# Dealing the first 713 steps of a fused attention and expert kernel anew to five queues

## The chip, the cores and the metric

The kernel runs on one core of one Trainium2 chip. A core has five engines, each with an instruction queue of its own that it works through in order: TensorE (PE, matrix products), VectorE (DVE), ScalarE (ACT), GpSimd (POOL) and SyncE (SP, which issues transfers here). ACT and POOL issue transfers too. All transfers run on the core's 16 DMA engines. Matrix products are written to PSUM banks, and DVE or ACT must read a bank before another product may overwrite it. The metric is the device time of one execution in microseconds.

## The reference

There are two stages. First a linear attention over q, k and v of shape 8 x 8 x 576 x 64 (batch, heads, sequence, width), then a mixture of 4 experts that every one of the 4608 tokens passes through.

```python
phi = lambda x: np.where(x > 0, x, np.exp(x) - 1.0) + 1.0
kv = np.einsum('bhsd,bhse->bhde', phi(k), v)
z = np.sum(phi(k), axis=2)
num = np.einsum('bhsd,bhde->bhse', phi(q), kv)
den = np.einsum('bhsd,bhd->bhs', phi(q), z)[..., None] + 1e-06
x = (num / den).transpose(0, 2, 1, 3).reshape(4608, 512)
p = domain_probs / (domain_probs.sum(-1, keepdims=True) + 1e-09)
for e in range(4):                      # w1: 4 x 512 x 1024, w2: 4 x 1024 x 512
    out += p[:, e:e + 1] * (np.maximum(x @ w1[e], 0.0) @ w2[e])
```

## The kernel before

The tokens are worked on in 9 tiles of 512. Tile j below 8 is the first 512 positions of batch j; the last 64 positions of all eight batches ("left-overs") make tile 8. Batch j+1's attention is computed beside tile j's experts. Only for batch 0 is there nothing to run beside it, so its attention, at the very start, is cut into many small pieces.

The work is a set of named steps. Each is a function or a generator; a generator yields between its parts, and each part belongs to one engine. The names that matter here, a digit i being the pair of heads or the quarter:

- batch 0's attention: `lq`, `lk`, `lv` load (line 548 and line 540; `CFG["LQ"]` and its like say which engine issues; lq3 and lk0 are ACT's, the others SP's). `ke`, `qe` are the exponentials on ACT (lines 563 and 581), `kl`, `ql` the linear part (566, 584) and `km`, `qm` the minimum of both (570, 587) on DVE, ql2 on POOL. `vc` casts v (573: vc0 and vc3 on POOL, vc1 on DVE, vc2 on ACT). `kv` is the 64 x 65 product (606) and two copies out of PSUM (617). `qT` turns phi(q) by PE and copies it on ACT (597). `nd` is numerator and denominator (628) and their quotient on DVE (631, 632). `xT` turns the result (642) and copies it (644).
- `L` with a group of hidden columns and a token half: expert 0's first layer of tile 0, two products of four matmuls (655), then a relu on ACT (664).
- `warm0` to `warm4`: 14, 3, 2, 1 and 5 matmuls on zeros (997), which keep PE busy while it would wait. They are the fillers.
- `w` with layer, expert and part: a weight's load with a cast, issued by POOL (lines 224 to 230). `k`, `v`, `q` with a digit: raw loads of batch 1 by POOL (319). `rk`, `rv`: its left-overs, in two halves (297).
- `p1` to `p7` and `c22`, with tile, expert and half: a block of a first layer, done with seven products instead of eight. p1 writes bank b, ACT copies it to a bank e; p2 adds to e, and ACT takes the relu of it (901); p5 overwrites the same bank e; p6 and p7 add to b, with copies to `u2` and `u3` on ACT (879); c22 adds u3 to e on DVE (852); p3 adds to e, p4 to b. `s` and `t` are the sums of weights that they need (DVE), `ts` the sums of tokens (DVE for tile 0, POOL for later ones).
- `y` with expert, token quarter and part: the second layer of tile 0 (715); `m` with tile and expert: that of later tiles, also by seven products (810), for which `hs` on POOL makes hidden sums (777 to 783).
- `b1.` and `b2.`: the attention of batches 1 and 2, with `b1.k0` and its like the two parts of phi on ACT (344, 347), `km`, `qm` the minimum on DVE (352), `v0` a cast of v on ACT (357), `lk`, `lv`, `lq` the left-overs (375 to 381), `kv`, `qT`, `nd`, `xT` as above. `load` and `next` are loads that SP issues.

Each of four tags has two PSUM banks, and u3 has a single buffer.

What sets the order: `CFG["EARLY"]` is a text of names. `advance` (line 1107) takes each name in turn and runs the step's next part, whose instructions go to the end of their engine's queue. So the text is dealt to five queues, and only the order within one queue has an effect, with the buffers' turns. After the text, at the start of expert 0 of tile 2, all that is left follows by due positions that the change leaves alone. A name that stands two or three times is one step's successive parts; below a prime marks the second part (qT0' is the copy of qT0) and two the third.

Of the kernel before, what the change touches and what calls it, by code (L numbers as in the profile page):

```python
# [84 lines left out]
    "WARM": (14, 3, 2, 1, 5),  # L85
    "BANK": {'qT0': 'py', 'qT1': 'b', 'nd00': 'py', 'nd00+': 'b', 'kv2': 'py', 'xT00': 'b', 'kv3': 'b', 'nd10+': 'b', 'L00': 'b', 'L10': 'py', 'nd01': 'b', 'xT01': 'py', 'nd11+': 'b', 'L20': 'e', 'L30': 'e', 'L01': 'e', 'L11': 'py', 'L21': 'py', 'L31': 'b', 'b1.qT3': 'py', 'b1.nd30': 'py', 'b1.nd21': 'b', 'b1.q1': 'b', 'b1.qT1': 'py', 'b1.nd01': 'py', 'b1.xT2': 'b', 'b1.nd11': 'py', 'b1.xT0': 'b'},
    "EARLY": (
# [31 lines left out]
    ),  # L119
}  # L120

# [1029 lines left out]
```

## Time and profile before

| | us |
|---|---|
| median of 3 runs | 485.68 (485.55 to 485.99) |
| the profiled execution | 485.38 |
| its span, first to last instruction | 483.6 |
| PE busy in the span | 474.8 |
| end of the part that the text orders, on PE | 117.8 |
| mean granted TensorE clock | 0.997 |

Engine rows give busy time, its share and the number of instructions. Timeline rows give start and length in microseconds, engine, line, operation, output and inputs with their shapes, and in brackets how long the engine had been idle and what ended that. A DMA row's length is its issue alone; when the data land is recorded apart. PE's rows overlap: the next matmul starts before the last has left the array.

### The profile page before, as it was taken

The page shows a single profiled execution, that of the slowest core. Times are in us where ns is not written, and L with a number is a line of the kernel's source. Part 1 is how long each engine was busy: PE and PEld are TensorE (multiplying, and loading weights), DVE is VectorE, ACT ScalarE, POOL GpSimd, SP SyncE. Part 2 cuts the span into 40 slices and gives each one's busy share as a digit, 9 for nine tenths or more (in the row PEclk, how much of TensorE's full clock was granted, in tenths as well). Part 3 has the DMA queues.
Part 4 walks back from the last instruction along what each step waited for, and adds up shares of the span by engine and source line. Part 5 has one row for each costly group of instructions (what it writes and reads, how often), then busy time and mean ns, then how long its engine had stood idle before and what let it go on. Part 6 is the DMA issues. An engine that isn't in the chain of part 4 may idle for free.

```text
span 483.6 us, 12013 instructions
## 1 busy us (share of the span) xinstructions
PE 474.8 (98%) x4565; PEld 407.5 (84%) x4565; DVE 377.8 (78%) x794; ACT 331.7 (69%) x662; POOL 357.5 (74%) x343
## 2 busy tenths in 40 slices
PE   7899999999999999999999999999999999999996
PEld 3776766898889888998899888988898888888885
DVE  5768988997868895888679876988687756775686
ACT  4688989956895599649874888478944565446530
POOL 5565044789866986799678977697769877987775
PEclk9999999999999999999999999999999999999998
DMA  8999986443445254524552346323221020002003
GB/s 292 219 218 255 232 209 211 122 111 83 133 143 110 45 159 152 109 51 124 171 128 56 115 138 158 71 82 102 75 59 23 7 94 2 1 0 89 2 1 87
DMA packets 79945, 53.67 MB, mean 111 GB/s; under 512 B 45152, under 2 KB 72608, under 8 KB 79888
## 3 DMA queue, kind: packets, MB, share of 16 engines
q1 hardware_dynamic: 69760, 40.43, 30.2%
q0 software_dynamic: 8896, 11.47, 12.3%
q10 hardware_dynamic: 1232, 1.02, 0.7%
q8 instruction: 35, 0.57, 0.5%
q14 instruction: 22, 0.18, 0.1%
HBM read 45.16 MB, written 9.44 MB: 113 GB/s over the span
## 4 chain that ended last, share of the span: by engine, by line
PE 96%; DVE 1%; DMA 1%; issue 0%; ACT 0%; SPq 0%; DVEq 0%
PE py L810 39%; PE pb L868 25%; PE pe L868 19%; PE py L715 6%; PE ph L655 1%; PE psum_nd L472 1%; PE psum_kv L444 1%; DMA rawq<-in_q_dram 1%; PE pb L810 1%; PE pe L810 1%; DVE kpos L566 0%; PE psum_nl L490 0%; PE psum_num L628 0%; DVE qp L587 0%; PE warm_ps L997 0%
## 5 line engine op out<-in xcount | busy, mean ns | idle before, releaser
L706 DVE SCALAR_TENSOR_TENSOR acc<-py,p_sb,acc 128x256 f32<-128x256 f32 (+1 forms) x382 | 182.5, 489 | 42.5 <-PE py L810 39.0
L852 DVE CUSTOM_DVE_ANT_0 h<-pe,u 128x512 f16<-128x512 f32 x140 | 96.2, 689 | 45.7 <-PE pe L868 27.1
L868 PEld LDWEIGHTS <-w 128*128 128x128 f16 x1120 | 108.9, 98 | 16.2
L777 POOL TENSOR_TENSOR hs<-h 128x512 f16<-128x512 f16 x64 | 74.6, 1165 | 56.8 <-DVE h L852 53.0
L810 PEld LDWEIGHTS <-h 128*128 128x128 f16 x1024 | 99.6, 98 | 11.3
L810 PE MATMUL py<-w,h 128*128 128x256 f16 x744 | 106.4, 273 | 0.0
L879 ACT COPY u<-pb 128x512 f32<-128x512 f32 x140 | 82.3, 590 | 29.7 <-PE pb L868 27.7
L779 POOL TENSOR_TENSOR hs<-hs,h 128x512 f16<-128x512 f16 x64 | 74.0, 1156 | 26.2 <-PE py L810 23.7
L868 PEld LDWEIGHTS <-s 128*128 128x128 f16 x840 | 81.3, 98 | 12.1
L868 PE MATMUL pb<-tt,w 128*128 128x256 f16 x560 | 83.8, 273 | 0.0
L810 PEld LDWEIGHTS <-hs 128*128 128x128 f16 x768 | 74.4, 98 | 8.8 <-issue 0.2
L783 POOL TENSOR_TENSOR hs<-h,hs 128x512 f16<-128x512 f16 x64 | 74.4, 1163 | 0.9 <-PE py L810 0.9
L810 PE MATMUL py<-t,hs 128*128 128x256 f16 x496 | 74.1, 273 | 0.0
L781 POOL TENSOR_TENSOR h<-h 128x512 f16<-128x512 f16 x64 | 73.9, 1155 | 0.1
L901 ACT ACTIVATE h<-pe 128x512 f16<-128x512 f32 x70 | 41.9, 599 | 41.2 <-PE pe L868 40.3
L894 ACT COPY pe<-pb 128x512 f32<-128x512 f32 x70 | 40.1, 573 | 41.8 <-PE pb L868 15.8
L922 ACT ACTIVATE h<-pb 128x512 f16<-128x512 f32 x70 | 41.8, 599 | 6.5 <-PE pb L868 6.3
L868 PE MATMUL pe<-tt,s 128*128 128x256 f16 x280 | 42.0, 273 | 0.0
L868 PE MATMUL pb<-tt,s 128*128 128x256 f16 x280 | 41.8, 273 | 0.0
L868 PE MATMUL pe<-xT,s 128*128 128x256 f16 x248 | 37.1, 273 | 0.0
L868 PE MATMUL pb<-xT,w 128*128 128x256 f16 x248 | 37.1, 273 | 0.0
L868 PE MATMUL pe<-xT,w 128*128 128x256 f16 x248 | 37.0, 273 | 0.0
(133 smaller groups left out, 595.9 us busy)
## 6 DMA issues: line engine op xcount, KB each, us to landing
out_dram<-acc SPq DMA_DIRECT2D x32, 256.0 KB, 2.5
w<-in_moe_w_dram POOLq DMA_DIRECT2D x14, 512.0 KB, 10.5
rawb<-in_k_dram SPq DMA_DIRECT2D x24, 256.0 KB, 3.0
rawb<-in_q_dram SPq DMA_DIRECT2D x24, 256.0 KB, 2.7
rawb<-in_v_dram SPq DMA_DIRECT2D x24, 256.0 KB, 2.8
w<-in_moe_w_dram POOLq DMA_DIRECT2D x4, 256.0 KB, 5.5
rawb<-in_k_dram POOLq DMA_DIRECT2D x4, 256.0 KB, 10.4
rl<-in_q_dram SPq DMA_DIRECT2D x16, 64.0 KB, 2.8
```

Source lines behind the costliest of these rows:

```text
L706: nc.vector.scalar_tensor_tensor(out=acc, in0=ps, scalar=pscal, in1=acc, op0=AO.mult, op1=AO.add)
L777: nc.gpsimd.tensor_tensor(out=hs[0], in0=a21, in1=a22, op=AO.add)
L779: nc.gpsimd.tensor_tensor(out=hs[1], in0=hs[0], in1=a11, op=AO.subtract)
L781: nc.gpsimd.tensor_tensor(out=a21, in0=a11, in1=a21, op=AO.subtract)
L783: nc.gpsimd.tensor_tensor(out=hs[3], in0=a12, in1=hs[1], op=AO.subtract)
L810: nc.tensor.matmul(out=ps, lhsT=lhsT(k), rhs=rhs[:, k], start=first and k == 0, stop=k == FH - 1, skip_group_check=True,)
L852: nc.vector._custom_dve(TENSOR_ADD_SAT, out=out, in0=ps, in1=u, s0=BIG, s1=0.0)
L868: nc.tensor.matmul(out=ps[:, kk], lhsT=lk(kc), rhs=rhs[:, kc], start=first and kk == 0 and kc == 0, stop=kc == 1, skip_group_check=True,)
L879: nc.scalar.copy(u, self.b)
L894: nc.scalar.copy(self.e5, self.b)
L901: nc.scalar.activation(self.h[:, :, 0, 0:NH], self.e5, AF.Relu)
L922: nc.scalar.activation(self.h[:, :, 1, 0:NH], self.b, AF.Relu)
```

## The change

The 713 names of the text keep their number and their meaning; each queue holds the same parts as before. Their order in the text, and so on the queues, is another. The five fillers stand where they stood on PE, around qT0, qT2, kv0 and nd01. These are the first parts on each queue, before and after:

```
SP    before lq2 lq0 lk1 lpr0 lv0 lv1 lk2 lk3 lv3 lv2 lq1
      after  lq2 lq0 lk1 lk3 lv0 lk2 lv1 lq1 lv3 lpr0 lv2
POOL  before ql2 vc0 w100 w102 w103 vc3 w101 w110 w111 k3 w200 rk1 w201 v0 rv0 rk0 v1 rv1 w120 w121 w210
             w211 v2 k0 k2 q1 k1 v3 q0 w130 w131 q3 w220 q2 w221 w231 w230 ts1.0
      after  ql2 rv0 vc0 rv1 w102 w100 vc3 w101 w103 w110 w111 w200 w201 k0 w120 k3 w121 k2 w210 k1 rk1
             rk0 w211 v0 v2 v1 v3 q3 q1 w130 w131 q0 w220 w221 q2 ts1.0 w230 w231
ACT   before lq3 lk0 qe0 ke0 qe2 ke1 qe3 qT0' qT2' kv0' kv0'' kv1' ke2 ke3 vc2 xT01' xT11' qT3' qe1 kv3'
             kv3'' kv2'' xT00' xT10' qT1' L01'' L31''
      after  lk0 ke0 qe2 lq3 qe0 ke1 ke3 qT2' ke2 kv0' kv0'' kv1' qT0' qe1 qe3 vc2 b1.lv kv3' kv3'' xT10'
             xT00' kv2'' qT3' xT11' qT1' xT01' L01''
DVE   before ql0 ql3 qm0 kl0 km0 qm2 kl1 km1 qm3 vc1 kl2 kl3 kv1'' nd01' km2 km3 nd00' ql1 kv2' qm1 nd11'
             xT21' xT31' nd10' ts0.2 ts0.0
      after  kl1 qm2 ql0 qm0 kl0 km0 km1 vc1 ql3 kl3 kv1'' km3 kl2 nd01' km2 nd00' qm3 ql1 qm1 kv2' nd11'
             nd10' ts0.0 xT21' xT31' ts0.1
PE    before warm0 qT0 warm1 qT2 warm2 kv0 warm3 kv1 nd01 warm4 xT11 xT01 qT3 nd00 kv3 kv2 xT00 L01 nd11
             xT10 L31 qT1 L10 xT21 xT31 L11 nd10 L01' L31' L00 xT30 xT20 L20 L30
      after  warm0 qT0 warm1 qT2 warm2 kv0 warm3 kv1 nd01 warm4 nd00 kv3 xT01 xT10 xT00 kv2 qT3 xT11 qT1
             L30 nd11 L10 nd10 L01 xT21 L00 L31 xT31 L11 xT20 L01' L31' xT30
```

The diff replaces the whole text; these are lines of it that the queues above do not show.

```diff
     "EARLY": (
...
-        "p2.010 s1.1 L20 w121 p2.010 p1.011 L21 L21 L21 s1.2 p6.010 p5.010 w210 L11 s1.3 p6.011 y0.30 p2.011 p6.010 p7.010 w211 p7.010 s0.1 p6.011 c22.010 v2",
...
-        "w131 p5.021 b1.v2 q3 b1.lkm y1.11 p6.021 b1.k0 b1.k2 b1.k1 w220 t1.1 t1.2 p7.021 y1.12 p7.021 c22.020 p3.020 y1.23 b1.v3 b1.km0 p4.020 p4.020 y1.00",
-        "y1.01 q2 w221 y1.13 p4.021 b1.km2 b1.km1 b1.kv c22.021 p3.021 y1.02 y1.03 p1.030 p4.021 b1.q1 y1.30 y1.13 b1.load1 p1.031 b1.q0 p3.020 y1.31 p3.021",
...
-        "p3.030 b1.nd11 b1.nd10 p7.031 y2.00 y2.01 b1.nd30 p5.031 p4.031 p4.030 b1.next b1.nd31 b1.nd30 y2.20 b1.load0 b1.xT0 b1.lq b1.lqm b1.nd31 b1.q2 b1.qm2",
...
-        "b1.xT1 p3.030 b1.nd21 y2.03 b1.xT0 b1.nd20 b1.nd21 y2.23 y2.10 y2.11 ts1.0 p1.101 p1.101 b1.load5 t1.3 b2.load0 t2.0 b1.xT2 y2.12 y2.13 b1.xT2 b2.k1",
...
+        "s1.0 s1.1 w131 p1.010 L21 p1.011 L10 L21 L30 L20 p1.010 p2.010 q0 p1.011 p2.010 w220 p2.011 s1.2 ts0.2 s1.3 p5.010 L21 L10 p6.010 p6.011 y0.00 y0.30",
...
+        "p7.020 b1.k1 t1.0 b1.km0 c22.020 b1.km2 y1.11 p7.021 c22.021 b1.km1 b1.lk p4.020 b1.lkm y1.12 b1.v0 b1.v2 p4.020 y1.13 p4.021 y1.21 y1.22 p3.020 y1.23",
+        "b1.v1 b1.v3 p4.021 b1.q1 p3.020 b1.kv y1.23 y1.13 p3.021 y1.00 p3.021 b1.kv b1.q3 b1.qm1 y1.01 y1.02 y1.03 q2 y1.03 b1.qT1 b1.qm3 b1.qT1 p1.031 p1.030",
...
+        "b1.nd01 t2.0 b1.nd00 b1.q2 y2.01 y2.02 b1.nd00 y2.03 p4.031 s3.2 b1.qm2 y2.03 c22.031 b1.xT0 y2.20 y2.21 y2.22 b1.qT2 b1.nd31 y2.23 p3.030 y2.23",
...
+        "y2.12 p1.100 b1.xT3 b1.nd21 b1.nd20 ts1.0 w230 w231 b1.xT2 y2.30 y2.13 y2.31 y2.32 p1.101 y3.10 b2.k2 p3.030 b1.xT3 p3.031 y2.13 b1.xT2 b1.lq p1.100",
...
+        "s0.2 y2.33 t0.3 b2.km0 p1.101 p6.101 p2.101 y3.12 p2.100 p7.100 p4.100 y3.13 p5.100 b2.v2 p6.101 t2.1 c22.100 y3.13 b2.k1 p2.101 y3.30 y3.31 p5.101",
...
```

51 rows, old and new, of the table nl are left out of this document.

## The prediction

> **What bounds the kernel now.** I read the page first (busy times, chain), then the busy time by stretch, then the timeline of the first 65 us, since only the order of the first 117 us of TensorE work is changed.
>
> ```profile
> PE 474.8 (98%) x4565; PEld 407.5 (84%) x4565; DVE 377.8 (78%) x794; ACT 331.7 (69%) x662; POOL 357.5 (74%) x343
> ...
> PE 96%; DVE 1%; DMA 1%; issue 0%; ACT 0%; SPq 0%; DVEq 0%
> ```
>
> ```profile
> core 0: us, PE busy (x) PEld busy (x) DVE busy (x) ACT busy (x) POOL busy (x), PEclk, DMA share, GB/s
> 0.00:8.00 8.00, 6.42 (x20) 2.39 (x21) 3.15 (x9) 3.01 (x5) 3.01 (x11) 1.00 0.74 255
> 8.00:12.00 4.00, 2.76 (x50) 1.42 (x48) 3.90 (x8) 2.81 (x9) 3.98 (x6) 1.00 1.09 368
> 12.00:16.00 4.00, 2.97 (x61) 2.02 (x60) 3.20 (x9) 3.20 (x7) 4.00 (x7) 1.00 1.24 205
> 16.00:20.00 4.00, 3.65 (x48) 3.21 (x49) 2.78 (x8) 1.97 (x7) 1.75 (x3) 1.00 1.15 212
> 20.00:40.00 20.00, 20.00 (x157) 15.02 (x156) 15.25 (x29) 16.44 (x33) 9.85 (x14) 1.00 1.21 220
> 40.00:60.00 20.00, 20.00 (x192) 14.19 (x190) 18.13 (x36) 19.63 (x41) 5.85 (x8) 1.00 1.15 252
> 60.00:120.00 60.00, 60.00 (x551) 48.01 (x549) 52.32 (x107) 46.76 (x97) 40.25 (x36) 1.00 0.57 150
> ```
>
> PE (TensorE) is the bound: it idles 1.2 us before its first fillers, some 3.0 us between 7 and 17 us, and not at all from 20 to 240. From 17 us on, every step starts where the last ends: four matmuls of 256 columns 0.437 us, two of 512 columns 0.433. PE's work is the same in any order, so the time changes by one thing alone: PE's idle time after, less PE's idle time now. All that can be won lies before 17 us (with the half-empty starts some 4.0 us); any stall that the new order puts behind it is lost whole. The other two facts: ACT is full from 40 to 60 (19.63 of 20), and DMA is saturated until about 65.
>
> ```profile
> 8.43 2.38 POOL L227 DMA_DIRECT2D w<-in_moe_w_dram  x3
> 12.43 0.23 DVE L617 CAST kvz<-psum_kv 64x65 f16<-64x65 f32 x1
> 16.01 0.28 PE L642 MATMUL psum_xh<-identh,x_sb 128*128 128x128 f16 x2 [0.33 <-DVE x_sb L632]
> 25.10 0.60 PE L868 MATMUL pe<-xT,w 128*128 128x256 f16 x4
> 25.79 0.60 ACT L901 ACTIVATE h<-pe 128x512 f16<-128x512 f32 x1
> 26.84 0.60 PE L868 MATMUL pe<-tt,s 128*128 128x256 f16 x4
> 64.77 1.16 POOL L849 TENSOR_TENSOR tt<-xT 128x512 f16<-128x512 f16 x1 [17.35 <-ACT xT L516]
> ```
>
> The three rows from 25.10 are p2.010, its relu, and p5.010, which overwrites the bank that the relu reads. Now 1.74 us lie between the two PE steps.
>
> **The change, part by part.** Durations are of the profiled execution (485.38 us, span 483.6), 0.30 below the median of the runs; I add the difference to the median. Hand-overs cost 0.05 to 0.09 us in the rows.
>
> *First loads.* lq3's load moves on ACT behind ke0 and qe2, lk0's ahead. ACT then issues lq3 at about 5.9 instead of 0.74; the engines' bandwidth is shared (DMA share 1.09), and in this trace the loads land 0.63 or 0.75 us apart from 6.3 to 12.1. lq3, which now lands at 4.7, lands after nine others: I take 10.5, between 9.4 (the two queues share evenly from the start) and 11.2 (strict order of issue). DVE's ql3 stands behind vc1 (lv1 at 9.5, cast to 10.2): it waits 0.3. For sharing speaks that a load that ACT issued at 1.28 landed (6.03) ahead of one that SP issued at 1.26 (6.25). [...]
>
> *DVE from ql3 to xT31'.* By rows: ql3 0.4, kl3 0.57, kv1'' 0.2 (ends 11.7; now 12.66), km3 and kl2 1.0, nd01' 0.93 (ends 13.65; now 13.99), km2 0.41, nd00' 0.93 (15.0; now 15.95), qm3, ql1, qm1 1.2 (16.2), kv2' 0.2. ACT then copies kv2'' and qT3' (16.65, 17.25), PE does nd11, DVE nd11' (17.85 to 18.8), nd10' (to 19.7), ts0.0, xT21', xT31' (20.6). PE: xT10 waits for nd00' from 13.9 to 15.05, L30 for qm1 and the xT copies until 16.5, nd11 until 17.3; from 18.6 it runs through. The second half of L01 then starts at about 20.85 and ends at 21.29. Now it ends at 20.05, but with L00, L30 and xT20 (0.437 + 0.437 + 0.12 = 1.0) not yet done: 21.05 for equal work. The front costs +0.25. Ends: DVE's 8.5 us of rows after 10.2 without one wait puts it at 18.95 (-1.65); lq3 at 11.2, and casts beside a busy POOL at 0.65 instead of 0.45 each, +1.0.
>
> *b1.lv on ACT ahead of kv3'.* It needs both halves of the left-over v, issued by POOL at 6.4 and 8.4. The first weight issued by POOL (256 KB, 8.43) landed 4.9 us after issue; four times as large as a half. With 4.9 the second lands at 13.3, ACT reaches it at 13.85: nothing. Cover is thin, see the rivals.
>
> *p2.010, p2.011, p5.010.* Now one PE step lies between p2.010 and p5.010. From p2's start: 0.60 until its last matmul is out, 0.09 hand-over, 0.60 relu, 0.06: 1.35. Two steps take 0.87. p5.010 stalls +0.48, whatever the front does; all other p2-p5, p1-p2 and p6-p7 pairs of the new order that I walked have 1.3 us or more. Bounds 0.40 to 0.60.
>
> *24 to 47 us.* I set each ACT and DVE queue against PE's steps (ACT 0.48 to 0.52 from start to start, 1.05 for a two-part phi, 0.60 an acc; DVE 0.605). The tight places: p3.010 behind c22.010 (0.1 spare), y0.10 behind y0.33' (0.0), p2.020 behind p1.020' (short by 0.06), b1.qT3 behind b1.qm3 (short by 0.1). Together +0.15, 0 to 0.6.
>
> *b1.kv.* It moves 0.8 us forward on PE, while b1.v0, v2, v1, v3 move behind b1.k1, p7.021' and b1.lk on ACT. From p1.020' ACT has 11.1 us of rows without a pause before b1.v3 is done; PE needs 10.9 from the same point to b1.kv and 11.5 to its last pair. Casts for pairs 1 and 3 come late: +0.3, 0 to 0.7. The v loads, now behind w211 on POOL's queue, land by 44 (the 17 loads behind the first weights summed at 2.5 us a weight piece, 0.65 a raw one), ACT wants them at 46: nothing.
>
> *w230 and w231* move on POOL behind ts1.0, which waits for both transposes of b1.xT0 and xT1. Now both are issued by 47.4, and land at 62.1 and 64.9. After, ts1.0 starts at about 62.4 (now 64.77, because xT0 and xT1 come earlier), ends at 63.6, and w230 follows. A weight of half the size took 4.9 from issue, the other half costs 1.25: it lands at 69.8, and y3.10, now first of its matrix, wants it at 69.35: +0.45, 0 (it is issued earlier) to 1.5 (the loads of batch 2 on SP share the engines; 0.57 of DMA is in use from 60 to 120). w231 has a second to spare.
>
> *The rest* (weights w120 to w221 earlier or later by up to 3 us on POOL, the six-deep raw loads and the stores on SP, POOL's hidden sums from 83 instead of 77, DVE's m steps) goes at nothing: w110/w111 land at 21 and 24, wanted at 24 and 26; w200 at 26.5, wanted at 28.8; the sums need 9.2 us of each 13.1 and have caught up by 92. Their cover is one to two us; if it is gone, a wait of that size appears under the line that reads them.
>
> Sum: 0.25 + 0.48 + 0.15 + 0.3 + 0.45 = 1.63. 485.68 + 1.63 = 487.3 us.
>
> **The rivals.** *Faster: DVE's front runs without waits.* If lq3 lands by 9.4 and nd11 and nd10 never keep DVE waiting, the front gains 1.65; with p5.010 at 0.48 and b1.kv and w230 at nothing, 484.5. It decides where the second half of L01 starts before about 19.3. For it: kv1'' and nd00' do come 0.9 earlier. Against: nd11 needs kv2'', which needs qm1, which is twelve DVE operations on.
>
> *Level.* The front gains 0.7 to 1.5 and pays for the stalls: 485.3 to 486.3.
>
> *b1.lv holds ACT.* POOL's left-over loads took 5.4 at least and 9.4 at the median from issue to landing, then behind weights:
>
> ```profile
> DMA to landing us min/median/max: 5.4/9.4/12.7
> ```
>
> At 9.4 the second half lands at 17.8; kv3', the xT copies and L30 stand behind it. Until 14.9 it costs nothing, then one for one: +2.9, 490.2. Against: here they are first in POOL's queue.
>
> *w230 late in full*, with the other terms: 488.4 to 489.3.
>
> That the change does nothing is excluded: the queues' own orders differ from the first load on.
>
> **How the numbers follow.** The forecast's case 0.50 (own range 486.4 to 488.2, from the ends of the small terms), w230 late or a few more stalls of the tight kind 0.13, b1.lv 0.05, level 0.20, faster 0.12. The range 485.2 to 489.3 leaves out most of faster and b1.lv. About 0.2%, 0.97 us, is what a measurement can tell from no change: slower takes the first three cases less a little (0.66), same the level case and the low edge of the first (0.22), faster 0.12.
>
> **What would show it.** Right: idle PE before p5.010 of about 0.5 us released by ACT's relu (line 901) near 27; short PE waits for vp (357) near 48 and for the weights' DMA near 69; the second half of L01 near 20.9. Wrong: ACT idle before line 381 near 14; DVE idle over a microsecond before its second line 584; PE idle elsewhere between 28 and 117, which would mean that a queue I called covered was not.

## The result, and the profile after

The changed kernel takes 490.85 us (median of 4 runs, 490.51 to 491.2), the kernel before, beside it, 485.81 us (485.55 to 485.99): a ratio of 1.0101, 95% interval 1.0087 to 1.0115. It is slower by 5.04 us. The forecast was 487.3 us (485.2 to 489.3): the sign was right, the size was not, and the time lies 1.55 us above the range. The profiled execution took 491.2 us with a span of 489.4.

The page of the changed kernel, TensorE's busy time and the chain of work that ended last. Before, the chain was TensorE's own to 96%, with 1% of transfers:

```profile
PE 477.7 (98%) x4565; PEld 408.0 (83%) x4565; DVE 379.2 (77%) x794; ACT 331.9 (68%) x662; POOL 358.9 (73%) x343
...
PE 79%; DMA 14%; DVE 3%; ACT 1%; POOL 1%; issue 1%; SPq 0%; ACTq 0%; DVEq 0%; POOLq 0%
```

Now transfers hold 14% of it, some 68 us. The chain itself shows where (start, length, what; its pieces between 25 and 76 us):

```profile
25.61 14.59 DMA w<-in_moe_w_dram
...
40.48 7.57 DMA rawv<-in_v_dram
...
48.61 14.43 DMA rawb<-in_q_dram
...
63.06 0.63 ACT qp L344
63.69 0.49 ACT psum_ee L347
64.18 0.52 ACT xT L516
...
64.79 1.15 POOL tt L849
65.94 0.73 POOL w L224
66.67 8.84 DMA w<-in_moe_w_dram
...
75.55 0.59 PE py L715 x2
```

Read from the top: w210 lands at 40.2, which lets POOL issue v3; v3 lands at 48.05, which lets it issue q2; q2 is issued at 48.6 and lands at 63.0; b1.q2 on ACT waits for it, the copy b1.xT0' stands behind b1.q2, ts1.0 needs that copy, w230 and w231 stand behind ts1.0, and y3.12 reads w231. Of these 50 us, 45 are transfers.

Why does w210 hold v3, and v3 hold q2? POOL's loads carry eight completion signals in turn (111 to 118 in both traces), and in both none of those that the text orders was issued before the one eight places ahead of it on POOL had landed; the closest came 0.28 us after. Their 34 loads landed in the order of issue, in both. w210 landed at 40.20 and v3 was issued at 40.48; v3 landed at 48.05 and q2 was issued at 48.61. So, as far as the two traces show, POOL's order sets not only in which order the bytes come, but also when each load can be issued at all. (When a load landed is read from its completion signal in the trace.)

TensorE's waits, in all (us, times, longest):

```profile
PE psum_num L628 <- DVE kvz L617: 1.6, 1, 1.6
PE psum_qT L595 <- DVE qp L587: 1.3, 1, 1.3
...
PE py L810 <- ACT acc L704: 0.7, 2, 0.5
PE py L715 <- DMA w<-in_moe_w_dram: 0.6, 1, 0.6
PE pb L868 <- ACT h L922: 0.4, 1, 0.4
PE py L715 <- DVE kp L352: 0.4, 1, 0.4
...
PE pe L868 <- ACT h L901: 0.3, 1, 0.3
```

The row `PE py L715 <- DVE kp L352` (0.4) is y3.10. DVE's step ended at 71.83 us and w230 landed at 71.79, so the two came within 0.04 us of each other; in the six other profiles with these loads, the row of y3.10 names the weight.

And the busy time by stretch, first of the changed kernel, then the last three stretches of the kernel before (columns: PE, PEld, DVE, ACT, POOL, the granted clock, the share of the DMA engines, GB/s):

```profile
12.00:16.00 4.00, 3.35 (x34) 1.88 (x34) 3.18 (x8) 1.49 (x3) 4.00 (x6) 0.57 1.18 186
40.00:60.00 20.00, 19.98 (x184) 13.71 (x183) 16.74 (x31) 19.16 (x39) 6.55 (x9) 1.00 1.19 247
60.00:65.00 5.00, 4.36 (x35) 2.61 (x33) 3.61 (x9) 3.95 (x8) 0.21 (x1) 1.00 0.32 99
65.00:70.00 5.00, 5.00 (x44) 3.45 (x44) 4.56 (x11) 2.73 (x6) 2.42 (x3) 1.00 0.86 150
70.00:75.00 5.00, 4.58 (x33) 2.84 (x32) 3.34 (x5) 4.38 (x11) 4.01 (x4) 1.00 1.14 228
```

```profile
60.00:65.00 5.00, 5.00 (x43) 3.06 (x41) 4.86 (x13) 3.54 (x7) 0.23 (x1) 1.00 1.03 190
65.00:70.00 5.00, 5.00 (x36) 3.16 (x35) 5.00 (x9) 4.09 (x9) 4.13 (x4) 1.00 0.97 304
70.00:75.00 5.00, 5.00 (x40) 3.58 (x39) 3.81 (x7) 5.00 (x11) 0.94 (x2) 1.00 0.38 65
```

Transfers are as full as before from 40 to 60 us (a share of 1.19 against 1.15). Then they stand nearly idle for five (0.32 against 1.03), while w230 and w231 sit on POOL behind ts1.0, and run full from 70 to 75 (1.14 against 0.38), when TensorE wants what they bring.

To place the loss, I took the start of each TensorE step from the timeline and set it against its length when nothing waits (0.437 us for four matmuls of 256 columns, and so on), in both kernels. The last matmuls of the text's part start at 122.62 us instead of 117.36, 5.26 later. (The spans differ by 5.8. Most of the rest is one wait of 0.46 us at line 810 near 350 us. The profile of before_kv1, which has the old order, has two such, of 0.55 and 0.48 us.) Where the time went, in this profile:

| place | lost, us | forecast |
|---|---|---|
| front, to the second half of L01 | 1.49 | 0.25 |
| ahead of p5.010 | 0.46 | 0.48 |
| tight places, 24 to 47 us | 0 | 0.15 |
| b1.kv | 0.31 | 0.30 |
| ahead of y2.02 (w221) | 0.81 | 0 |
| ahead of y3.10 and y3.12 (w230, w231) | 0.80 | 0.45 |
| 77 to 103 us: behind m10.11 (ahead of p1.120) 0.58, behind p3.120 (ahead of m11.21) 0.40, six small ones | 1.4 | 0 |

The table adds up, but the experiments show that its rows are not prices: taking one of them away gave some half a microsecond at most.

### The profile page after: what moved, and what is told of

The parts are those of the page before. It is cut to its first block, busy times and chain, and to the rows that moved or that the text cites. A ratio compares the mean times of both kernels' runs of the same rounds, so it can differ in the third digit from the quotient of the medians.

```text
span 489.4 us, 12012 instructions
## 1 busy us (share of the span) xinstructions
PE 477.7 (98%) x4565; PEld 408.0 (83%) x4565; DVE 379.2 (77%) x794; ACT 331.9 (68%) x662; POOL 358.9 (73%) x343
## 4 chain that ended last, share of the span: by engine, by line
PE 79%; DMA 14%; DVE 3%; ACT 1%; POOL 1%; issue 1%; SPq 0%; ACTq 0%; DVEq 0%; POOLq 0%
PE py L810 38%; PE pb L868 21%; PE pe L868 16%; DMA w<-in_moe_w_dram 7%; DMA rawb<-in_q_dram 3%; DMA rawv<-in_v_dram 2%; DMA vrawt<-in_v_dram 1%; PE psum_nd L472 1%; DVE h L852 1%; PE psum_kv L444 1%; DMA rawq<-in_q_dram 1%; DVE acc L706 1%; PE pb L810 1%; PE pe L810 1%; PE psum_nl L490 0%
## 5 line engine op out<-in xcount | busy, mean ns | idle before, releaser
L810 PEld LDWEIGHTS <-hs 128*128 128x128 f16 x768 | 74.4, 98 | 8.6 <-issue 0.2
```

Source lines behind the costliest of these rows:

```text
L810: nc.tensor.matmul(out=ps, lhsT=lhsT(k), rhs=rhs[:, k], start=first and k == 0, stop=k == FH - 1, skip_group_check=True,)
```

## The experiments

The kernel before ran beside every group; differences are medians against it in the same group, to be held against 5.04. The runs of the kernel before spread by 1.1 to 2.7 us within a group.

### Two halves: front_new and front_old

```diff
 front_new
-"EARLY": the new text
+"EARLY": the new text up to the first p1.010, then what is left of the old text in the old order
 front_old
+"EARLY": the old text up to p1.011, then what is left of the new text in the new order
```

> All queues in the new order up to the first p1.010, everything behind it in the old order. Theory A, the losses sit where the trace shows them: only the front's excess stays (8.26 - 6.77 = 1.5 us), some 487.3 us; p5.010, b1.kv, y2.02, y3.10 and the steps behind 77 us as before. Rival B, the weights that POOL issues 1 to 3.5 us later from the front on are what starves the later stages: most of the 5.04 us stays, 489.3 us or more, and TensorE waits for a weight at y2.02.

> The old order up to p1.011, everything behind it in the new order. Theory A: the front's 1.5 us come back, the rest stays (p5.010 0.46, b1.kv 0.31, y2.02 0.81, y3.10 0.80, behind 77 us 1.4): 485.8 + 3.8 = 489.6 us, less what weights issued earlier give back at y2.02 (down to 488.8). Rival B: with the weights on time most of it is gone, 487 us or less.

front_new took 495.96 us (+10.09), front_old 497.90 us (+12.03). Each half is far worse than the whole, so neither theory's sum holds, and nothing is learned of the front's price. What is learned is why: each seam has ACT wait for a left-over load that the one half's POOL order brings late and the other half's ACT order takes early. From front_new (start, length, engine, line, operation; in brackets the idle time ahead and what ended it):

```profile
41.29 0.84 ACT L375 ACTIVATE kz<-rl 64x256 f16<-64x256 f32 x2 [4.02 <-DMA rl<-in_k_dram]
```

In front_old it was b1.lv, with 7.34 us ahead of it. ACT's order and POOL's order of loads belong together.

### The front: fill, lq3_first and the changed kernel once more

```diff
 fill
-    "WARM": (14, 3, 2, 1, 5),
+    "WARM": (14, 3, 2, 6, 5),
 lq3_first, ACT's queue
-lk0 ke0 qe2 lq3 qe0
+lq3 lk0 ke0 qe2 qe0
```

> The new order with the fourth filler 6 matmuls long instead of 1, so that TensorE works where it idled for 1.62 us ahead of the second half of nd01. Theory C, idle TensorE at 6.6 and at 11 us made the clock fall to 0.57 between 12 and 16 us: the clock stays at 1.00, the 5 matmuls of the last filler take 1.24 us instead of 2.29, and the time falls by 1.0 to 1.4, to 489.6 us. Rival D, TensorE waits for DVE there anyway, and a slow filler costs nothing: 490.8 us, and if the filler delays kv1 by more than its cover, 491.1 us.

> The new order with lq3's load again ahead of lk0's on ACT, as before the change. Theory E, lq3's late landing (11.52 us) holds DVE for 1.34 us and through it nd01: ql3 does not wait, kv1'' comes at about 11.2 instead of 12.37, TensorE's gap ahead of nd01's second half is under 0.7 us, the clock stays at 1.00, and the time falls by 1.5 to 2 us, to 489.1 us. Rival F, one load more ahead of the others delays lk0, lk1 and lv by as much as it gives: 490.5 to 491 us, with idle DVE before its first operations instead.

> The changed kernel itself once more, for the spread of its front. Theory P, the granted clock at 12 to 16 us and the landing of the first loads differ from run to run: the end of the front (L30) moves by 0.5 us or more against the first profile (18.86 us), while the end of the text's part moves by less than half of that, since weights hold it. Rival Q, the clock falls to 0.57 at the same place in every run of this order, and the front ends at 18.8 to 18.9 us. Time 490.5 to 491.2 us in both.

fill: 491.63 us (+5.76). In its profile the clock stayed at 1.00 from 8 to 20 us and the gap ahead of nd01's second half shrank to 0.3, as theory C says, but the time did not fall (and the second profile of the changed kernel, below, has 1.00 without the longer filler). lq3_first: 490.38 us (+4.51); DVE's wait went, the front ended 0.93 us earlier than in the first profile, and 0.5 us came out, a third of what theory E expected. The changed kernel once more: 491.11 us (+5.07). TensorE's rows of its two profiles, the first profile:

```profile
12.92 2.29 PE L997 MATMUL warm_ps<-qz 128*128 128x512 f16 x5
28.75 0.60 PE L868 MATMUL pe<-tt,s 128*128 128x256 f16 x4 [0.31 <-ACT h L901]
62.23 1.02 PE L715 MATMUL py<-w,h 128*128 128x512 f16 x4 [0.64 <-DMA w<-in_moe_w_dram]
71.83 0.60 PE L715 MATMUL py<-w,h 128*128 128x512 f16 x2 [0.42 <-DVE kp L352]
```

and the second:

```profile
11.73 1.24 PE L997 MATMUL warm_ps<-qz 128*128 128x512 f16 x5
26.60 0.60 PE L868 MATMUL pe<-tt,s 128*128 128x256 f16 x4 [0.31 <-ACT h L901]
28.41 1.02 PE L715 MATMUL py<-w,h 128*128 128x512 f16 x4 [0.33 <-DMA w<-in_moe_w_dram]
48.19 0.32 PE L444 MATMUL psum_kv<-vp,kp 128*64 128x65 f16 x8 [0.25 <-ACT vp L357]
52.62 1.05 PE L868 MATMUL pb<-xT,w 128*128 128x256 f16 x8 [0.73 <-DMA w<-in_moe_w_dram]
62.27 1.02 PE L715 MATMUL py<-w,h 128*128 128x512 f16 x4 [0.56 <-DMA w<-in_moe_w_dram]
72.23 0.61 PE L715 MATMUL py<-w,h 128*128 128x512 f16 x2 [0.77 <-DMA w<-in_moe_w_dram]
```

This is the most telling comparison of the study. The same program has TensorE 2.15 us earlier at p5.010 (26.60 against 28.75), its fillers at full clock (1.24 against 2.29 us), and it starts y2.02 at the same time. On the way it waits for weights where the first did not: 0.73 us at p1.031. Theory P holds, Q falls, and with it the clock as the cause: what the front wins, the weights take. The same in all seven profiles with these loads behind the front:

| kernel | front ends (nd11 starts, behind L30) | y2.02 starts | w221 landed | y3.10 starts |
|---|---|---|---|---|
| changed, first | 18.86 | 62.23 | 62.2 | 71.83 |
| changed, again | 16.71 | 62.27 | 62.2 | 72.23 |
| sums_early | 16.86 | 62.91 | 62.9 | 72.57 |
| t_late | 17.58 | 62.40 | 62.4 | 71.94 |
| lq3_first | 17.93 | 61.49 | 61.4 | 71.48 |
| p5_back | 18.30 | 62.76 | 62.7 | 72.51 |
| fill | 18.36 | 62.35 | 62.3 | 72.04 |

The front's end moves over 2.15 us, y2.02 follows w221 to within 0.1, and the one does not go with the other: the two earliest fronts have neither the earliest y2.02 nor the earliest y3.10. So the 3.07 us that the first profile had lost when y2.02 started (1.49, 0.46, 0.31 and 0.81 of the table) are set by w221: whatever TensorE wins ahead of it, it waits for there or at an earlier weight.

### One wait at a time: p5_back, loads_pool, w23_early

```diff
 p5_back, TensorE's queue
-p5.010 p6.010 p6.011 y0.00
+p6.010 p6.011 p5.010 y0.00
 loads_pool, in load(), line 304
+            self.loads = getattr(self, "loads", 0) + 1
+            if self.b == 2 and self.loads <= 4:
+                eng = nc.gpsimd
 w23_early, POOL's queue
-w221 q2 ts1.0 w230 w231 ts1.1
+w221 q2 w230 w231 ts1.0 ts1.1
```

> The new order with p5.010 moved behind p6.011 on TensorE, nothing else. Both theories: the wait of 0.46 us ahead of p5.010 goes, and TensorE is 0.46 us earlier up to 60 us. Theory G, each wait is lost whole: the end of the text's part comes at 122.2 instead of 122.6, 490.4 us. Rival H, the waits behind it end at times that the transfers set (w221 landed at 62.2 us whatever TensorE did): the wait at y2.02 grows from 0.81 by the same 0.46, and the time stays at 490.8 us.

> The new order, the first four raw loads of batch 2 (b1.load2, b1.load5, b2.load0, b1.load3) issued by POOL behind q2, so behind w221, instead of by SP from 38 us on. Theory I, they take the transfers' time ahead of w221: w221 lands at 59.5 to 60.5 instead of 62.2 us, TensorE does not wait at y2.02, the time falls by 0.8 to 490.0 us if nothing behind it takes this back, and 490.4 us if w230 does in part. Rival J, w221 is late because POOL issued every weight late from the front on: w221 lands at 61.5 us or later, y2.02 waits 0.5 us or more, 490.8 us.

> The new order with w230 and w231 issued ahead of ts1.0 again, behind q2. They are issued near 49 us instead of 65.9, land near 66 and 69 us instead of 71.8 and 75.5, and TensorE does not wait at y3.10 and y3.12. Theory G: the 0.8 us come back, 490.0 us. Rival K, the loads that SP issues from 53 us on then land later and hold the phi of batch 2 (ACT waits for raw k near 72 us): the time stays, or TensorE waits at b2.kv instead, 490.6 us or more.

p5_back: 491.27 us (+5.58). The wait at p5.010 is gone, and TensorE waits at p1.031 (0.95), y2.02 (0.63) and y3.10 (0.73) instead: rival H. The 0.46 us is real in its place and worth nothing in the sum.

loads_pool: 491.47 us (+5.78), from 489.32 to 493.79. In the profiled run, the slowest, the front was 2.6 us later than in the first profile, and w221, issued at 47.1 as in the first profile (47.2), landed at 59.1 instead of 62.2: theory I on the cause, rival J out. (That y2.02 does not wait says nothing here. With a front 2.6 us later TensorE would have come there behind 62.2 too.) But the time did not fall, since w230 stayed behind ts1.0 and y3.10 now waits 1.40 us:

```profile
74.58 0.60 PE L718 MATMUL py<-w,h 128*128 128x512 f16 x2 [1.40 <-DMA w<-in_moe_w_dram]
```

The spread says the same once more. Where weights hold TensorE, the changed kernel's eight runs lie within 1.0 us (490.51 to 491.53). Here, where w221 holds nothing, five lie within 4.5. That fits a front that differs from run to run and is no longer hidden, but there is one profile of the five.

w23_early: 490.49 us (+4.80). No wait at y3.10 or y3.12, and none at b2.kv, so rival K is out. Of the 0.8 us some 0.25 came out, less than these groups can tell from nothing. Its profile had the front late again (granted clock 0.65 from 16 to 20 us), so it does not show whether y2.02 would have taken the rest.

### DVE's sums of weights: t_late and sums_early

```diff
 t_late, DVE's queue
-... b2.qm0 t3.1 t2.3 y3.23' ... b2.qm3 t2.2 b2.qm2 ... t1.2 t3.3 ...
+... b2.qm0 y3.23' ... t1.2 ... t2.3 t2.2 p3.121' ... t3.1 t3.3 t3.2 ...
 sums_early, DVE's queue
-s0.2 y2.33' t0.3 b2.km0 t2.1 c22.100 y3.13' b2.km1 p3.100' t1.1 b2.km3 ... t1.3 ... t2.3 ... t2.2 ... t1.2
+b1.nd31' t1.1 ... y2.13' t1.3 b1.lqm b2.km2 t1.2 s0.2 y2.33' ... y3.13' t2.2 b2.km1 p3.100' t2.3 b2.km3
```

> The new order with four of DVE's sums of weights (t2.3, t2.2 and t3.1, t3.3, 0.7 to 1.7 us each piece) moved from between 87 and 99 us to behind the drains, near 115 us. Theory L, these sums hold DVE and through it the phi of batch 2 and the drains of PSUM on ACT: the waits between 84 and 103 us (1.4 us in all) shrink to under 0.4, the time falls by 1.0 to 1.4, to 489.6 us. Rival M, the hidden sums of POOL that start at 86.6 instead of 76.6 us, or the order of ACT itself, hold the m steps: the waits stay at 1 us or more, 490.8 us, and if the sums are missed behind 115 us a new wait of up to 1 us appears there.

> The new order with five of DVE's sums of weights moved from 80 to 97 us to where DVE idles ahead of them (t1.1, t1.3, t1.2 into 62 to 73 us, t2.2, t2.3 into 76 to 81 us), so that fewer run beside POOL's hidden sums, which start at 86.6 us. Theory L2, beside a POOL pass such a sum takes 1.0 to 1.65 us instead of 0.68, and this holds DVE's drains: the wait of 0.58 us at m10.11 and those at p2.110 and p3.110 go (0.8 us), the one at p3.120 (0.4) may stay, 490.0 us. Rival M2, the waits are ACT's order alone: they stay, and DVE's fuller stretch adds a new wait at y3 or p3.100, 491 us or more.

t_late: 496.98 us (+11.29). Theory L was right on the place: the waits behind m10.11 (0.58) and p3.110 (0.11) went, the 0.40 behind p3.120 stayed. But DVE has no room behind 110 us either: TensorE waits 1.26 and 3.26 us there, and the kernel is 6 us slower. sums_early: 490.73 us (+4.69). The waits behind m10.11, p2.110 and p3.110 went here too, and new ones of 0.47 at p7.100 and 0.22 and 0.25 around b2.kv took most of it; 0.35 us at most came out. So the sums hold the drains (L2): in the first profile t3.1 and t2.3 (0.69 and 1.65 us on DVE) stand ahead of b2.qm3, ACT's next phi waits 0.63 us for that up to 91.90, and the relu that p1.120 waits for (line 922) stands behind it on ACT. But a place where they hold nothing was not found. How long a sum takes on DVE is told in the last section.

### Together: late_mended, all_mended, k2_later and k2_later_b

```diff
 late_mended: loads_pool + sums_early, and POOL's queue
-w221 q2 ts1.0 w230 w231
+w221 q2 w230 w231 (b1.load2 b1.load5 b2.load0 b1.load3) ts1.0
 all_mended: late_mended + lq3_first + p5_back
 k2_later: all_mended, and ACT's queue
-b1.qT2' b2.k2 b1.xT3' b1.xT2' b1.lq p1.100' b2.k0
+b1.qT2' b1.xT3' b1.xT2' p1.100' b1.lq b2.k2 b2.k0
 and DVE's queue
-t1.3 b1.lqm b2.km2 t1.2 s0.2
+t1.3 t1.2 s0.2 b1.lqm b2.km2
 k2_later_b: k2_later, and DVE's queue
-y2.13' t1.3 t1.2 s0.2 b1.lqm b2.km2 y2.33' ... y3.13' t2.2 ... p3.100' t2.3
+y2.13' b1.lqm b2.km2 s0.2 y2.33' ... y3.13' t1.3 ... p3.100' t1.2
```

> The new order with three mendings behind 38 us at once: four raw loads of batch 2 issued by POOL behind w231, w230 and w231 ahead of ts1.0, the sums as in sums_early; the front, p5.010 and b1.kv stay as the change put them. Theory N, these transfers and sums are the 3.0 us that the prediction missed or had at half: TensorE does not wait at y2.02, y3.10 and y3.12, the text's part ends near 120.2 instead of 122.6 us, 488.4 us. Rival, the steps in between are as tight, and other waits take their place: 490 us or more.

> late_mended with lq3 ahead of lk0 on ACT and p5.010 behind p6.011 as well. Theory H (early time is lost only while transfers pin the steps behind it): with the transfers out of the way the 0.9 us of the front and the 0.46 us of p5.010, which gave 0.5 us and nothing when tried alone, now come out whole: 1.4 us below late_mended, 487.0 us. Rival O, early time is lost for another reason, such as ACT and DVE being full from 40 to 60 us: at most 0.5 us below late_mended. In neither is it faster than the kernel before.

> all_mended with one more step moved: b2.k2 (the phi of batch 2, which waits for a raw load until 68 us) behind the copies of b1.xT3, b1.xT2 and p1.100 on ACT. Theory N2, ACT's wait of 4.4 us there is what took back the mended 2 us: TensorE's wait of 1.6 us at p1.101 and that of 0.4 at p6.100 go, 487.4 us. Rival O2, the transfers are behind by that much in any order, and the wait moves to b2.kv or to p2.100: 489 us or more.

> k2_later with DVE's order mended: b1.lqm and b2.km2 ahead of the sums t1.3, t1.2 and s0.2, which held ACT's next phi for 2.6 us there (each 0.95 to 1.64 us beside POOL's sums of tokens); t2.2, t2.3 back where the change put them. Theory N2: with no raw load and no sum ahead of the copies, TensorE does not wait between 52 and 76 us, the wait at m10.11 (0.6) comes back, 488.0 us. Rival O2, a wait of 2 us or more appears at another step, since the transfers are behind in any order: 489.5 us or more.

late_mended: 491.38 us (+5.34), 489.88 to 493.27. No weight is waited for any more: w221 lands at 57.9, w230 at 61.5. In their place 0.7 us are lost ahead of p7.100, as the theory's rival has it. So the transfers and sums by themselves gave nothing: TensorE's own path is nearly as long. all_mended: 489.38 us (+3.34), 2.0 below late_mended. That is theory H's way and not O's: with no weight to wait for, the early time that gave 0.5 us and nothing alone comes out. But it rests on four runs each, those of late_mended spread over 3.4 us, and the two sets overlap, so the size is open. What is left shows on ACT, in all_mended:

```profile
68.19 0.63 ACT L347 ACTIVATE kp<-rawb 128x512 f16<-128x512 f32 x1 [4.40 <-DMA rawb<-in_k_dram]
```

The four raw loads now lie behind the weights and land from 65.4 to 68.1 us, and the new order has b2.k2 ahead of the copies that p1.101 waits for (1.6 us). k2_later moves it: that wait went, as did p6.100's, but the time rose to 492.10 us (+6.11). It moves more than the one step of its expectation: its text also has t1.2 and s0.2 on DVE ahead of b1.lqm, where all_mended had t1.3 alone. The three sums (0.95, 1.64 and 1.64 us, shown in the last section) held ACT's next phi, TensorE lost 3.4 us at p7.100, and its granted clock was 0.50 from 74.4 to 77.8 us, behind that wait. k2_later_b moves the sums away: 488.94 us (+2.84), without a wait between 52 and 66 us, but with 1.06 us at p7.100 and 0.59 and 0.40 behind m10.11 and p3.120. It lies between N2's 488.0 and O2's 489.5. All the mendings together (transfers, sums, lq3, p5.010, b2.k2) brought 2.2 of the 5.04 us back. The text's part of its profile ends 3.2 us later than before; they stand in the front (0.4), b1.kv (0.3), b1.xT3 (0.2), p7.100 (1.06) and from 77 us on (1.3).

### The front by itself: front_old_loads and front_old_loads_lq3

```diff
+"EARLY": the new text up to the first p1.010, its POOL names dealt in the old order and b1.lv left out,
+         then what is left of the old text in the old order
 front_old_loads_lq3, ACT's queue
-lk0 ke0 qe2 lq3 qe0
+lq3 lk0 ke0 qe2 qe0
```

> The new order of TensorE, ACT, DVE and of the first loads up to p1.010, but POOL's loads in the old order (and b1.lv where it was), and all steps behind p1.010 in the old order. Theory R, the change loses its 5 us by the order of the transfers behind the front, and the front by itself loses nothing: the stalls of 4.7 and 1.5 us of the run that took over POOL's new order too go, TensorE does not wait behind 24 us, and the time is that of before give or take what the front's landing differs, 485.0 to 487 us. Rival S, the front is worth its 1.5 us or more: 487.3 us or more.

> As front_old_loads, with lq3's load ahead of lk0's on ACT. With lq3 first the front ended at 17.9 us in two runs, behind lk0 at 16.7 to 21.5 us in ten. Theory R: 485.8 to 486.8 us, with a smaller spread than front_old_loads. Rival: if lq3's late landing costs DVE 1 us in every run, this one is faster than front_old_loads by 0.5 us or more, 485 us.

front_old_loads: 488.50 us (+2.51, ratio 1.0050, 1.0037 to 1.0062). The stalls of front_new are gone; the only wait of any size from 20 us to the end of the text's part is 1.07 at p2.010, which the seam makes. Without it, the new front costs some 1.4 us where nothing hides it: near rival S's 1.5. (An estimate: 2.51 less the 1.07 of one profile.) Theory R's first half, that the front by itself loses nothing, falls. front_old_loads_lq3: 487.64 us (+1.65, 1.0022 to 1.0045), the same seam in it: by the medians lq3's place in ACT's queue is worth 0.86 us of the 1.4, though the two intervals overlap. Its spread, 1.7 us over seven runs, is no smaller than the 1.2 of front_old_loads over five.

### A faster kernel: before_kv1

```diff
 the kernel before, DVE's queue
-vc1 kl2 kl3 kv1'' nd01'
+vc1 kl2 kv1'' kl3 nd01'
```

> The kernel before with one step moved: kv1'' on DVE ahead of kl3. It is a try at a faster kernel. From the profile of before: kl2 and kl3 end at 12.39, kv1'' at 12.66, and TensorE waits 0.75 us for it ahead of the second half of nd01; PE's kv1 is done by 11.7. If the front sets the time there (TensorE does not idle behind 20 us, and weights land ahead of their use), DVE's whole queue behind it comes 0.3 to 0.5 us earlier and the time falls by as much, 485.4 us; if kl3's delay of 0.25 us is handed on by km3 and kv3, it is level, 485.8 us.

485.40 us (11 runs) against 486.10 (14 runs), a ratio of 0.9982, 0.9972 to 0.9992. It is the only kernel here that is faster than the one before, by about what can be told at all. Its profiled run was the slowest of the eleven; its second half of nd01 starts at 12.56 instead of 12.71. An earlier front that gives time where TensorE waits for no weight would fit. No profile shows it: in this one the text's part ends 0.1 us later than in that of before.

## Why the prediction was wrong, and where it was right

**Right.** TensorE's work stays the same (4565 matmuls in both) and time is lost by waiting. Nothing could be won behind 17 us. p5.010 lost 0.46 us where 0.48 was said, with ACT's relu (line 901) as the releaser; b1.kv lost 0.31 where 0.30 was said; y3.10 waited until w230 had landed. b1.lv did not hold ACT: its halves landed at 11.8 and 12.9, before the forecast 13.3, and line 381 started at 13.36 without a wait. The tight places of 24 to 47 us cost nothing in the first profile.

**Not by idle time alone.** The forecast had the time change by TensorE's idle time and nothing else. On the pages, TensorE is busy 2.9 us longer (477.7 against 474.8) of the 5.8 us of span. 1.05 us of it are the last filler at half the clock (2.29 against 1.24). The rest was not placed; a part is that the last matmul ahead of a wait shows its whole length (0.60 for four, against 0.437 from start to start).

**The step that failed is "The rest ... goes at nothing".** It named the weights w120 to w221 and SP's raw loads, and checked w110, w111 and w200 alone. The weights that mattered came after: w130 landed at 52.5 instead of 48.1 us, w131 at 55.1 instead of 51.3, w220 at 59.0 instead of 55.5, w221 at 62.2 instead of 59.6. Before, SP's queue moved one raw load of 256 KB between 38 and 59 us; after, five, because b1.next no longer stands ahead of them. With four of these behind w221 it landed at 57.9 to 59.1 (late_mended, loads_pool). TensorE sat idle for these weights 0.64 us at y2.02 in the first profile (0.81 lost with the last matmul's tail); in the second, whose front was 2.15 us earlier, 0.73 at p1.031 and 0.56 at y2.02. The sentence "if it is gone, a wait of that size appears" was the right one, and its work was not done.

**w230.** The mechanism was right, the size not: 0.80 instead of 0.45, with w231's 0.22 in it, which was said to have a second to spare. ts1.0 started at 64.79, not 62.4; from issue to landing w230 then took 5.9 us where 6.15 was said, so it was the start that failed. The forecast took the transposes of b1.xT0 and b1.xT1 from TensorE's order, and missed that ACT's copy of b1.xT0 stands behind b1.q2, which waits for q2; q2 now lies behind w221 on POOL, and landed at 63.0 instead of 56.1. No run moved q2 alone; this link is read from the chain.

**The front.** 0.25 was said, with ends of -1.65 and +1.0; the first profile lost 1.49, the second gained some 0.7 on the kernel before, and where it is exposed it costs some 1.4 (the estimate above). lq3 landed at 11.52 us in the first profile, past the forecast's late end of 11.2, and held DVE for 1.34 us instead of 0.3. The early end, 9.4, was the author's estimate for two queues that share evenly from the start, and the first profile does not show that. ACT's queue moved no packet from 3.3 to 8.2 us, though lq3 was issued at 4.29, while SP's moved 1532; from 8 to 10 us it moved 486 beside 621 of SP's. So the two did move side by side, but from 3.9 us after the issue on. The granted clock was not in the sum at all.

**Hidden sums and m steps** went at nothing too, and cost 1.4 us of waits between 77 and 103 us, 0.7 of it behind steps that moving DVE's sums freed.

**The sum itself.** The forecast added the terms as if TensorE alone carried the time. Behind 25 us the changed kernel has a second path, from transfer to transfer, that ends later than TensorE's own, at y2.02 and at y3.10. Terms on the shorter path are not added but hidden: p5.010 and lq3's wait in the front gave 0 and 0.5 us when taken away alone. The two must be nearly equal, since taking away the longer one alone gave nothing either (late_mended). Of the terms on the longer path, w230 alone was in the sum. The range could not help: its upper end was w230 late in full on top of the other terms, and no case held a late w221 or waits behind 77 us.

**Open.** That w221 sets the time up to 62 us, and that SP's raw loads make it late, is shown. How the 5.04 us divide is not: 2.84 us stay in the best mending. Which of them belong to the order of ACT and DVE alone, and whether some order of the loads serves both the weights and batch 2's raw data in time, was not found out.

## What to carry to other kernels

Find out how many loads an issuing queue lets be under way, here eight on POOL, where v3 was issued 0.28 us after w210 had landed. Where the DMA engines are full, here with a share of 1.19 from 40 to 60 us, make a list of every load with its place in the order of bytes and the time of its first use, before and after, to the end of the full stretch, not only for the first few. Here w221 landed at 62.2 us with five raw loads on SP's queue, at 57.9 to 59.1 with four of them behind it, and with w230 and w231 behind a wait on POOL the share was 0.32 from 60 to 65 us. A wait that the profile shows is worth its length only if no second path ends at the same place (the 0.46 us at p5.010 gave nothing): two profiles of one kernel with different luck early on tell this for free. An order of steps on one engine and the order of the loads that feed it are one decision; here half of each lost 10.09 and 12.03 us, the whole new order 5.04.

## What was not expected of the hardware

**The clock fell with short gaps, and not in every run.** In the first profile the granted clock was 0.57 from 12 to 16 us though TensorE's longest gaps before it were 1.34 and 1.62 us. That mean is half the clock for 3.41 us and the full clock around them:

```profile
9.02:12.43 3.41, 2.01 (x46) 1.20 (x44) 2.04 (x6) 3.13 (x8) 1.88 (x3) 1.00 1.13 340
12.43:15.84 3.41, 3.19 (x24) 1.72 (x25) 2.65 (x7) 1.06 (x3) 3.41 (x6) 0.50 1.16 184
15.84:19.25 3.41, 2.93 (x65) 2.21 (x62) 2.05 (x6) 2.30 (x8) 3.41 (x5) 1.00 1.00 126
```

In the second profile of the same kernel, with gaps of 1.2 and 0.44, it was 1.00; with one gap of 3.1 us (lq3_first) it was 1.00 too; with 3.3 us (loads_pool) it was 0.50 from 8.5 to 18.8 us, three times 3.41. In the nine profiles that have such a fall ahead of the program's end, it is always to 0.50 and lasts 3.41 us or two or three times as long. In the 3.41 us ahead of a fall TensorE was busy 59% of the time in the first profile (2.01 of 3.41) and 35% in loads_pool. That alone does not decide: in lq3_first it was busy 10% of the 3.41 us from 5.40, and the clock stayed. What decides was not found out.

**The front differs from run to run**, and the granted clock in it: 0.57 and 1.00 from 12 to 16 us in the changed kernel's two profiles. With lq3 behind lk0 the front's end (the start of nd11, behind L30) lay between 16.7 and 21.5 us in eleven profiles of nearly the same front; with lq3 ahead, four of five lay at 17.8 to 17.9, the fifth at 18.9.

**A sum of weights on DVE took 0.68 or 0.69 us alone and up to 1.65 beside POOL's sums, and POOL's took longer too.** Of the 32 sums of weights in the changed kernel's first profile, the 25 with no sum of POOL beside them took 0.68 or 0.69 us each, the other seven 0.69 to 1.65. In k2_later, DVE's three sums

```profile
68.75 0.95 DVE L771 TENSOR_TENSOR w<-w 128x1024 f16<-128x1024 f16 x1
69.62 1.64 DVE L769 TENSOR_TENSOR t<-w,t 128x1024 f16<-128x1024 f16 x1
71.18 1.64 DVE L752 TENSOR_TENSOR s<-w,s 128x1024 f16<-128x1024 f16 x1
```

lie beside three of POOL:

```profile
68.00 1.15 POOL L852 TENSOR_TENSOR tt<-xT,tt 128x512 f16<-128x512 f16 x1 [4.50 <-ACT xT L519]
69.11 1.60 POOL L852 TENSOR_TENSOR tt<-xT 128x512 f16<-128x512 f16 x1
70.67 1.60 POOL L852 TENSOR_TENSOR tt<-xT,tt 128x512 f16<-128x512 f16 x1
```

Both take longer side by side: 1.64 instead of 0.68 on DVE, 1.60 on POOL instead of 1.15 (at 64.79 us in the changed kernel, with no sum of DVE's beside it). One after the other at the shorter lengths, a pair would take 1.83 us (an estimate, 0.68 and 1.15); the rows show 1.60 to 1.64. What makes them longer is not shown. (The line numbers of this kernel are three higher, since `load` has three more lines.) In the changed kernel t2.3 takes 1.65 us at 88.3, beside POOL's hidden sums, where it took 0.68 at 76.4, and t3.3 1.64 instead of 0.69. The prediction did not price that.
